# Cross network on one core: a two-engine eviction, a load on another ring, a bias from a table, and other transfer sizes

## The chip, the cores and the metric

One core of a Trainium2 chip runs the whole kernel. The metric is device time in microseconds (us) from launch to end, lower is better. A profiled execution also has a span: from the first to the last instruction on the core.

The engines are TensorE (PE in the profile; its weight loads are PEld), VectorE (DVE), ScalarE (ACT), GpSimd (POOL) and SyncE (SP). SP computes nothing here; its queue issues transfers. ScalarE's queue can issue transfers too, on a ring of its own, in order with ScalarE's computing instructions. Each engine works its instructions off in program order, and waits where an operand isn't ready.

## The reference

Six layers of a cross network over 4096 rows of 416 values, all in bf16:

```python
B, F, D, L = 4096, 26, 16, 6
Din = min(F * D, 1024)          # 416
x0: (B, Din)   ws: (L, Din, Din)   bs: (L, Din)

def reference(x0, ws, bs):
    x = x0
    for l in range(ws.shape[0]):
        x = x0 * (x @ ws[l] + bs[l]) + x
    return x
```

In the first layer x is x0, so the kernel computes x0 * (x0 @ w + (b + 1)) there and saves the addition.

## The kernel before, in words

**Layout.** In layers 0 to 4 x lies transposed: features on the 128 partitions, rows of the batch along the free dimension. The 416 features are three full blocks of 128 (the tiles XM, index m or k) and a remainder of 32 (XR). The 4096 rows are two half-batches s of 2048, each four groups g of 512 columns (CW). Since the remainder has 32 features only, its four groups of one half-batch lie under each other on the 128 partitions: XR[32g:32g+32, 512s:512s+512]. XRx is the same for one half-batch with its upper and lower halves exchanged. WM holds the weights of the full blocks, WR the 32 remainder rows of the weights four times under each other, WD the weights from remainder to remainder as a block diagonal.

**How x0 comes in.** Eight transposed loads on SP's queue (load_x0t, L78) fill XM[0], one for each 512 rows: (s, g) = (0,0), (0,1), ... (1,3). The remainder can't come that way. load_xrem (L83) loads it in three parts, in rows of 64 bytes, into xrem: rows 0 to 1023 on SP (64 KB), rows 1024 to 2047 on ScalarE's ring (64 KB, L275), and the third part, the whole second half-batch, on SP between the sixth and the seventh transposed load (128 KB, L116). x0_rem (L157 to L160) then transposes a part on VectorE in squares of 32 (xrem to xrt), copies it into XR in the right order, and copies XR's halves into XRx.

**First layer** (first_layer, L226 to L272). For each half-batch the columns are handled in two halves h, of two groups each. A block m of a half takes two of the eight PSUM banks (two_banks hands them out in the order of first_order). full (L232) runs three matmuls for each group, row (L239) adds the remainder's part from XR or XRx. Then the banks are emptied. split_first does it with both engines: ScalarE reads the first bank with the bias added (L178), VectorE reads the second with bias and multiplication in one instruction (L179), then multiplies ScalarE's half with x0 (L181). ew_main does it in one piece: ScalarE reads both banks (L166), VectorE multiplies (L169). Block 0 goes through split_first, blocks 2 and 1 through ew_main. The bank pair of block 0 and that of block 2 of the first half are the ones that blocks 1 and 2 of the second half take next. After the second half of the first half-batch, x0_rem(1, 0, 128) stands on VectorE ahead of the evictions of blocks 1 and 2.

**Layers 1 to 4.** Tiles (s, m), each four banks, with matmuls 32 columns wide in four column groups of TensorE (mm_full, L197), the remainder's rows (mm_row, L203) and the remainder's own output (mm_rem, L209 and L214). ScalarE empties two banks at a time with the bias (L166), VectorE multiplies with x0 (L171) and adds x (L172). In layer 4 each finished block is transposed back to rows by a transfer on SP (xl_dmat, L221) into XLrows.

**Last layer.** Here x is the stationary operand, so that rows come out on the partitions. Eight quads q of 4 x 128 rows: full matmuls (mm_q_full, L342), remainder rows (L351) and the bias (L356), which is a matmul with one row: ones times bLr, the last layer's biases, which a small load puts on partitions 0, 32, 64 and 96 (L125). ew_pair empties two groups at a time (L366), multiplies with X0rows (L367), adds XLrows (L368) and stores 208 KB on SP (L369). X0rows is x0 by rows, loaded in one transfer of 3328 KB at the end of SP's loads (L124). The last two quads go through ew_single, a group at a time (L376, L377, L380, L381).

**Small preparations.** bsb holds the six bias rows; VectorE transposes them (L101) and GpSimd spreads them into bM and bR (L103 to L107), then fills WD (L129). Filler matmuls (L146) run on TensorE until the first operands are there.

The order of all instructions is written out by hand; the framework only adds the waits that the operands need.

Of the kernel before, what the change touches and what calls it, by code (L numbers as in the profile page):

```python
# [10 lines left out]
ALU = mybir.AluOpType  # L11
BF16 = mybir.dt.bfloat16
# [4 lines left out]
def kernel(  # L17
# [7 lines left out]
    nc = tc.nc  # L25
    B, D = x0.shape
    L = ws.shape[0]
    P = 128
    NK = 3
    R = D - NK * P  # L30
    assert R == 32 and B == 4096 and D == 416 and L >= 2
    NS = 2
    NG = 4
    CW = 512
    SW = NG * CW
    NBT = B // P
    LL = L - 1
# [11 lines left out]

    dz = const.tile([P, 2], FP32)  # L50
    warm = const.tile([P, CW], BF16)
    ones = const.tile([P, P], BF16)
    WM = const.tile([P, L, NK, D], BF16)
    WR = const.tile([P, L, D], BF16)
    WD = const.tile([P, L, NG, R], BF16)
    bsb = const.tile([R, D], BF16)
    bT = const.tile([R, D // R, R], BF16)
    bLr = const.tile([P, D], BF16)
    bM = const.tile([P, NK, L], FP32)
    bR = const.tile([P, L], FP32)  # L60
    X0rows = big.tile([P, NBT, D], BF16)
    XLrows = big.tile([P, NBT, D], BF16)
    scrR = [big.tile([P, 4, P], BF16, name=f"scrR{s}") for s in range(NS)]
    xrt = [big.tile([P, 16, R], BF16, name=f"xrt{s}") for s in range(NS)]
    xrem = [big.tile([P, 16, R], BF16, name=f"xrem{s}") for s in range(NS)]
    XRx = [big.tile([P, CW], BF16, name=f"XRx{s}") for s in range(NS)]
    XM = [big.tile([P, NK, B], BF16, name=f"XM{i}") for i in range(3)]
    XR = [big.tile([P, NS * CW], BF16, name=f"XR{i}") for i in range(3)]
# [12 lines left out]
    def load_xrem(eng, s, p0, p1):  # L81
        with nc.allow_non_contiguous_dma(reason="64B row segments"):
            eng.dma_start(xrem[s][p0:p1], x0[SW * s + 16 * p0:SW * s + 16 * p1, NK * P:D].rearrange("(p t) r -> p t r", t=16))  # L83
# [4 lines left out]
    nc.vector.memset(warm[:, 0:P], 0.5)  # L88
    nc.vector.memset(warm[:, P:CW], 0.5)
    nc.vector.memset(dz[:], 0.0)  # L90
    nc.gpsimd.memset(bsb[:], 0.0)
    nc.gpsimd.memset(ones[:], 1.0)
    nc.gpsimd.memset(WD[:], 0.0)

    load_x0t(0, 0)
# [2 lines left out]
    load_wr(nc.scalar, 0, 0, 1)  # L98
    nc.scalar.activation(dz[:, 1:2], dz[:, 0:1], ACT.Identity, bias=dz[:, 0:1], scale=1.0)

    nc.vector.transpose(out=bT[:], in_=bsb.rearrange("p (c r) -> p c r", r=R))  # L101
    for q in range(4):
        nc.gpsimd.tensor_copy(bM[32 * q:32 * q + 32, :, :], bT[:, q:4 * NK:4, 0:L])  # L103
    nc.gpsimd.tensor_scalar(out=bM[:, :, 0:1], in0=bM[:, :, 0:1], scalar1=1.0, scalar2=None, op0=ALU.add)
    for g in range(NG):
        nc.gpsimd.tensor_copy(bR[32 * g:32 * g + 32, :], bT[:, 4 * NK, 0:L])
    nc.gpsimd.tensor_scalar(out=bR[:, 0:1], in0=bR[:, 0:1], scalar1=1.0, scalar2=None, op0=ALU.add)  # L107
    for g in range(1, NG):
        nc.vector.tensor_copy(WR[32 * g:32 * g + 32, 0, :], WR[0:32, 0, :])
    load_x0t(0, 1)  # L110
# [2 lines left out]
    load_x0t(0, 3)  # L113
    load_x0t(1, 0)
    load_x0t(1, 1)
    load_xrem(nc.sync, 1, 0, 128)  # L116
    load_x0t(1, 2)
    load_x0t(1, 3)
    load_wm(nc.sync, 1)
# [1 line left out]
        load_wr(nc.sync, g, 1, L)  # L121
    for l in range(2, L):
        load_wm(nc.sync, l)
    nc.sync.dma_start(X0rows[:], x0_v)  # L124
    nc.sync.dma_start(bLr[0:P:32, :], bs[LL:LL + 1, :].broadcast_to([NG, D]))  # L125

    def fill_wd(l0, l1):
        for g in range(NG):
# [24 lines left out]
    def x0_rem(s, p0, p1, parts):  # L153
        XRv = XR[0][p0:p1, CW * s:CW * s + CW].rearrange("p (j t) -> p j t", t=16)
        n = 16 // len(parts)
        for a, copy in enumerate(parts):
            nc.vector.transpose(out=xrt[s][p0:p1, n * a:n * a + n, :], in_=xrem[s][p0:p1, n * a:n * a + n, :])  # L157
            copy(XRv[:, :, n * a:n * a + n], xrt[s][p0:p1, n * a:n * a + n, :].rearrange("p t j -> p j t"))
        for a in range(p0, p1, 64):
            nc.vector.tensor_copy(XRx[s][64 - a:128 - a, :], XR[0][a:a + 64, CW * s:CW * s + CW])  # L160


    def ew_main(l, s, m, h, pt, cur, nxt):
        c0 = col0(s, 2 * h)
        t = tpool.tile([P, 2 * CW], BF16, name="t")
        nc.scalar.activation(t[:], pt.rearrange("p a b -> p (a b)"), ACT.Identity, bias=bM[:, m, l:l + 1], scale=1.0)  # L166
        x0c = XM[0][:, m, c0:c0 + 2 * CW]
        if l == 0:
            nc.vector.tensor_tensor(out=nxt[:, m, c0:c0 + 2 * CW], in0=t[:], in1=x0c, op=ALU.mult)  # L169
            return  # L170
        nc.vector.tensor_tensor(out=t[:], in0=t[:], in1=x0c, op=ALU.mult)  # L171
        nc.vector.tensor_tensor(out=nxt[:, m, c0:c0 + 2 * CW], in0=t[:], in1=cur[:, m, c0:c0 + 2 * CW], op=ALU.add)  # L172


    def split_first(s, m, h, pt, nxt):
        c0 = col0(s, 2 * h)
        t = tpool.tile([P, 2 * CW], BF16, name="t")
        nc.scalar.activation(t[:, 0:CW], pt[:, 0, :], ACT.Identity, bias=bM[:, m, 0:1], scale=1.0)  # L178
        nc.vector.scalar_tensor_tensor(out=nxt[:, m, c0 + CW:c0 + 2 * CW], in0=pt[:, 1, :], scalar=bM[:, m, 0:1],  # L179
                                       in1=XM[0][:, m, c0 + CW:c0 + 2 * CW], op0=ALU.add, op1=ALU.mult)  # L180
        nc.vector.tensor_tensor(out=nxt[:, m, c0:c0 + CW], in0=t[:, 0:CW], in1=XM[0][:, m, c0:c0 + CW], op=ALU.mult)  # L181

    def ew_rem(l, s, pr, curR, nxtR):
        tr = tpool.tile([P, 2 * CW], BF16, name="t")
# [41 lines left out]
    def first_layer(s):  # L226
        cur, nxt = XM[0], XM[1]

        def full(pt, m, h, gl, first, last):
            c0 = col0(s, 2 * h + gl)  # L230
            for k in range(NK):
                nc.tensor.matmul(pt[:, gl, :], lhsT=WM[:, 0, k, 128 * m:128 * m + 128], rhs=cur[:, k, c0:c0 + CW],  # L232
                                 start=(first and k == 0), stop=(last and k == NK - 1), skip_group_check=True)

        def row(pt, m, h, swapped, first):
            for gl in range(2):
                r0 = 32 * ((2 * h + gl + 2 * swapped) % 4)
                src = XRx[s][r0:r0 + 32, :] if swapped else XR[0][r0:r0 + 32, CW * s:CW * s + CW]
                nc.tensor.matmul(pt[:, gl, :], lhsT=WR[r0:r0 + 32, 0, 128 * m:128 * m + 128], rhs=src,  # L239
                                 start=first, stop=(not first), tile_position=(r0, 0), skip_group_check=True)  # L240

        pa = [two_banks() for m in range(NK)]
        for m, gl in ((0, 0), (1, 0), (2, 0), (0, 1), (1, 1), (2, 1)) if s == 0 else ((0, 0), (1, 0), (0, 1), (1, 1), (2, 0), (2, 1)):
            full(pa[m], m, 0, gl, True, False)
        pb = [two_banks()]
        row(pa[0], 0, 0, 0, False)
        if s == 1:
            row(pb[0], 0, 1, 0, True)
        row(pa[2], 2, 0, 0, False)
        row(pa[1], 1, 0, 1, False)  # L250
        split_first(s, 0, 0, pa[0], nxt)
        if s == 0:
            x0_rem(0, 64, 128, (nc.vector.tensor_copy,))
        for m in (2, 1):
            ew_main(0, s, m, 0, pa[m], cur, nxt)
        pb += [two_banks() for m in range(1, NK)]
        for m, gl in ((0, 0), (1, 0), (2, 0), (0, 1), (1, 1), (2, 1)) if s == 0 else ((0, 0), (1, 0), (0, 1), (1, 1), (2, 0), (2, 1)):
            full(pb[m], m, 1, gl, s == 0 or m > 0, s == 1 and m == 0)
            if s == 1 and (m, gl) == (0, 1):
                ew_main(0, s, 0, 1, pb[0], cur, nxt)  # L260
        if s == 0:
            row(pb[0], 0, 1, 0, False)
            row(pb[1], 1, 1, 0, False)
            row(pb[2], 2, 1, 1, False)
            split_first(s, 0, 1, pb[0], nxt)
            x0_rem(1, 0, 128, (nc.vector.tensor_copy,))
            for m in range(1, NK):
                ew_main(0, s, m, 1, pb[m], cur, nxt)
        else:
            row(pb[1], 1, 1, 0, False)  # L270
            row(pb[2], 2, 1, 1, False)
            rem_first(pb)  # L272
# [74 lines left out]
    def mm_q_rows(qs, pys, begun):  # L347
        for q, py in zip(qs, pys):
            s, i = quads[q]
            for g in range(NG):  # L350
                nc.tensor.matmul(py[g // 2][:, g % 2, 0:D], lhsT=curR[32 * g:32 * g + 32, CW * s + 128 * i:CW * s + 128 * i + 128],  # L351
                                 rhs=WR[32 * g:32 * g + 32, l, :], start=not (q == begun and g < 2), stop=False,
                                 tile_position=(32 * g, 0), skip_group_check=True)
        for q, py in zip(qs, pys):
            for g in range(NG):
                nc.tensor.matmul(py[g // 2][:, g % 2, 0:D], lhsT=ones[32 * g:32 * g + 1, :],  # L356
                                 rhs=bLr[32 * g:32 * g + 1, :], start=False, stop=(q == begun and g < 2), tile_position=(32 * g, 0),
                                 skip_group_check=True)

    def ew_pair(q, h, py):  # L360
        s, i = quads[q]
        b0 = 16 * s + 8 * h + i
        t = tpool.tile([P, 2 * CW], BF16, name="t")
        tv = t[:, 0:2 * D].rearrange("p (a d) -> p a d", a=2)
        o = opool.tile([P, 2, D], BF16, name="o")
        nc.scalar.copy(tv, py[h][:, :, 0:D])  # L366
        nc.vector.tensor_tensor(out=tv, in0=tv, in1=X0rows[:, b0:b0 + 5:4, :], op=ALU.mult)  # L367
        nc.vector.tensor_tensor(out=o[:], in0=tv, in1=XLrows[:, b0:b0 + 5:4, :], op=ALU.add)  # L368
        nc.sync.dma_start(out_v[:, b0:b0 + 5:4, :], o[:])  # L369

    def ew_single(q, g, py):
        s, i = quads[q]
# [64 lines left out]
```

## Time and profile before

| | |
|---|---|
| three runs | 130.89, 131.26, 131.39 us; median 131.26 |
| the profiled execution | 130.53 us |
| its span, first to last instruction | 128.7 us |
| granted TensorE clock | 1.0 |
| TensorE busy | 122.9 us, 95% of the span |
| VectorE busy | 104.2 us, 81% |
| ScalarE busy | 83.3 us, 65% |
| GpSimd busy | 7.0 us, 5% |
| largest groups | L197 on TensorE 65.2 us; L166 on ScalarE 59.1 us; L171 and L172 on VectorE 33.3 and 33.5 us |

The busy shares of TensorE, VectorE, ScalarE and the transfers, in 40 slices of 3.2 us each (a digit is tenths, 9 is 90% or more):

```profile
PE   6999999999999999999999999999999999999950
...
DVE  1344969457979898989898989898989999999990
ACT  2117358399757759766749666849666877567760
...
DMA  3989989999991000000000000000398899995663
```

The transfer engines are full from 3 to 38 us, while x0, the weights and X0rows come in, and busy again from 90 us on, with the transposes back and the stores. A group's line names its source line, engine and operation, what it writes from what it reads, how many there are, busy time in us and the mean of one in ns. In the timeline the first two columns are the start and the length in us; instructions of one kind that follow each other are merged into one line (x2 and so on). "Issued" is the moment an engine's queue starts a transfer, "landed" the moment at which whoever waits for it may go on.

### The profile page before, as it was taken

Reading aid. Unit: us, or ns where it says so; the run is one execution under the profiler, and the core shown is the slowest. Engines: PE = TensorE matmul, PEld = TensorE weight load, DVE = VectorE, ACT = ScalarE, POOL = GpSimd, SP = SyncE. Lnnn points to the kernel's source line nnn. Section 1 sums busy time; section 2 is a strip of 40 time slices with the busy share of each in tenths; the row PEclk is TensorE's granted clock in tenths of the full one; section 3 lists DMA queues with packets and bytes.
Section 4 is the critical chain, followed back from the end, with each engine's and each line's share of the span. In section 5 each row is a group of like instructions: output and inputs, shape, how many; then the busy total and the mean of one; then the engine's idle time right before and its main releaser. Section 6 shows DMA issues by size and latency. Waiting matters only on the chain.

```text
span 128.7 us, 3923 instructions
## 1 busy us (share of the span) xinstructions
PE 122.9 (95%) x1677; PEld 54.5 (42%) x1677; DVE 104.2 (81%) x187; ACT 83.3 (65%) x93; POOL 7.0 (5%) x27
## 2 busy tenths in 40 slices
PE   6999999999999999999999999999999999999950
PEld 3343334444434444544444444434444445544420
DVE  1344969457979898989898989898989999999990
ACT  2117358399757759766749666849666877567760
POOL 4250000030000000000000000000000300000000
PEclk9999999999999999999999999999999999999999
DMA  3989989999991000000000000000398899995663
GB/s 94 261 155 222 179 153 277 225 326 333 335 316 30 5 0 8 0 0 5 0 5 0 5 0 5 0 0 5 73 135 185 163 150 234 235 293 176 198 192 103
DMA packets 41973, 16.37 MB, mean 127 GB/s; under 512 B 30778, under 2 KB 41956, under 8 KB 41956
## 3 DMA queue, kind: packets, MB, share of 16 engines
q1 hardware_dynamic: 40456, 15.70, 54.8%
q10 hardware_dynamic: 1500, 0.42, 1.6%
q8 instruction: 13, 0.21, 0.7%
q14 instruction: 4, 0.03, 0.1%
HBM read 6.15 MB, written 3.41 MB: 74 GB/s over the span
## 4 chain that ended last, share of the span: by engine, by line
PE 93%; ACT 2%; DVE 2%; issue 1%; DVEq 0%; ACTq 0%
PE PS L197 49%; PE PS L342 12%; PE PS L232 12%; PE PS L203 5%; PE PS L214 5%; PE PS L146 4%; PE PS L209 2%; PE PS L351 2%; PE PS L239 1%; PE PS L356 1%; DVE t L377 1%; ACT t L166 1%; DVE o L380 1%; ACT t L178 1%; ACT t L376 0%
## 5 line engine op out<-in xcount | busy, mean ns | idle before, releaser
L166 ACT ACTIVATE t<-PS,bM 128x1024 bf16<-128x1024 f32 x57 | 59.1, 1115 | 21.2 <-PE PS L203 21.2
L197 PE MATMUL PS<-XM,WM 128*32 128x512 bf16 x1152 | 65.2, 379 | 0.0
L197 PEld LDWEIGHTS <-WM 128*32 128x32 bf16 x1152 | 29.8, 97 | 33.7 <-issue 5.1
L171 DVE TENSOR_TENSOR t<-t,XM 128x1024 bf16<-128x1024 bf16 x48 | 33.3, 694 | 4.2 <-ACT t L166 4.2
L172 DVE TENSOR_TENSOR XM<-t,XM 128x1024 bf16<-128x1024 bf16 x48 | 33.5, 698 | 3.1
L342 PE MATMUL PS<-WM,XM 128*128 128x416 bf16 x96 | 17.9, 340 | 0.0
L232 PE MATMUL PS<-XM,WM 128*128 128x512 bf16 x72 | 16.9, 385 | 0.2 <-ACT t L166 0.2
L366 ACT CAST t<-PS 128x832 bf16<-128x832 f32 x12 | 10.2, 852 | 5.0 <-PE PS L342 2.3
L342 PEld LDWEIGHTS <-XM 128*128 128x128 bf16 x96 | 8.9, 98 | 8.7 <-issue 2.2
L232 PEld LDWEIGHTS <-WM 128*128 128x128 bf16 x72 | 6.9, 99 | 10.1 <-issue 2.8
L214 PE MATMUL PS<-XM,WM 128*32 128x512 bf16 x120 | 8.2, 379 | 0.0
L185 ACT ACTIVATE t<-PS,bR 128x512 bf16<-128x512 f32 x10 | 6.8, 694 | 2.0 <-POOL WD L129 2.0
L368 DVE TENSOR_TENSOR o<-t,XLrows 128x832 bf16<-128x832 bf16 x12 | 7.1, 592 | 0.5
L203 PE MATMUL PS<-XR,WR 32*128 32x512 bf16 x96 | 7.3, 379 | 0.0
L169 DVE TENSOR_TENSOR XM<-t,XM 128x1024 bf16<-128x1024 bf16 x9 | 5.9, 688 | 1.5 <-ACT t L166 1.5
L367 DVE TENSOR_TENSOR t<-t,X0rows 128x832 bf16<-128x832 bf16 x12 | 7.0, 584 | 0.0
L146 PE MATMUL PS<-warm 128*128 128x512 bf16 (+2 forms) x13 | 4.6, 535 | 1.0 <-DVE warm L88 1.0
L178 ACT ACTIVATE t<-PS,bM 128x512 bf16<-128x512 f32 x3 | 2.1, 687 | 5.3 <-PE PS L239 5.3
L285 POOL COPY XLrows<-scrR 128x512 bf16<-128x512 bf16 x2 | 1.3, 666 | 72.7 <-DMA scrR<-XR 72.7
L157 DVE STREAM_TRANSPOSE xrt<-xrem 64x256 bf16<-64x256 bf16 (+2 forms) x4 | 2.2, 562 | 3.5 <-DMA xrem<-in_x_dram 3.5
L376 ACT CAST t<-PS 128x416 bf16<-128x416 f32 x8 | 4.0, 506 | 1.0 <-PE PS L342 0.8
L214 PEld LDWEIGHTS <-WM 128*32 128x32 bf16 x120 | 3.2, 97 | 3.2
(40 smaller groups left out, 48.1 us busy)
## 6 DMA issues: line engine op xcount, KB each, us to landing
X0rows<-in_x_dram SPq DMA_DIRECT2D x1, 3328.0 KB, 15.3
out_dram<-o SPq DMA_DIRECT2D x12, 208.0 KB, 2.6
WM<-in_ws_dram SPq DMA_DIRECT2D x5, 312.0 KB, 6.5
out_dram<-o SPq DMA_DIRECT2D x8, 104.0 KB, 1.7
WR<-in_ws_dram SPq DMA_DIRECT2D x4, 130.0 KB, 6.0
WM<-in_ws_dram ACTq DMA_DIRECT2D x1, 312.0 KB
XM<-in_x_dram SPq DMA_TRANSPOSE x8, 4.8
xrem<-in_x_dram SPq DMA_DIRECT2D x1, 128.0 KB, 4.4
```

The source lines that it names most:

```text
L146: nc.tensor.matmul(PS[:, 0, 0:cols], lhsT=warm[:, 0:P], rhs=warm[:, 0:cols], start=True, stop=True, skip_group_check=True)
L166: nc.scalar.activation(t[:], pt.rearrange("p a b -> p (a b)"), ACT.Identity, bias=bM[:, m, l:l + 1], scale=1.0)
L171: nc.vector.tensor_tensor(out=t[:], in0=t[:], in1=x0c, op=ALU.mult)
L172: nc.vector.tensor_tensor(out=nxt[:, m, c0:c0 + 2 * CW], in0=t[:], in1=cur[:, m, c0:c0 + 2 * CW], op=ALU.add)
L197: nc.tensor.matmul(pts[g // 2][32 * q:32 * q + 32, g % 2, :], lhsT=WM[:, l, k, 128 * m + 32 * q:128 * m + 32 * q + 32], rhs=cur[:, k, c0:c ...
L203: nc.tensor.matmul(pts[g // 2][:, g % 2, :], lhsT=WR[32 * g:32 * g + 32, l, 128 * m:128 * m + 128], rhs=curR[32 * g:32 * g + 32, CW * s:CW ...
L214: nc.tensor.matmul(pr[32 * g:32 * g + 32, :], lhsT=WM[:, l, k, NK * P:D], rhs=cur[:, k, c0:c0 + CW], start=False, stop=(k == NK - 1), tile ...
L232: nc.tensor.matmul(pt[:, gl, :], lhsT=WM[:, 0, k, 128 * m:128 * m + 128], rhs=cur[:, k, c0:c0 + CW], start=(first and k == 0), stop=(last ...
L342: nc.tensor.matmul(py[g // 2][:, g % 2, 0:D], lhsT=cur[:, k, q_cols(q, g)], rhs=WM[:, l, k, :], start=(first and k == 0), stop=((not first ...
L366: nc.scalar.copy(tv, py[h][:, :, 0:D])
L367: nc.vector.tensor_tensor(out=tv, in0=tv, in1=X0rows[:, b0:b0 + 5:4, :], op=ALU.mult)
L368: nc.vector.tensor_tensor(out=o[:], in0=tv, in1=XLrows[:, b0:b0 + 5:4, :], op=ALU.add)
```

## The change

It has five parts.

- In the first layer's first half of the first half-batch, blocks 0 and 2 both go through split_first, and block 1 through ew_main behind them (before: block 0 split, blocks 2 and 1 in one piece). split_first now returns its last multiplication, so that VectorE reads both banks out of PSUM before it multiplies ScalarE's halves.
- The remainder's third part is issued by ScalarE, behind its eviction of block 1, and no longer by SP between the transposed loads. The two xrem tiles become one.
- The last layer's bias comes from bsb: GpSimd copies its 32 rows to all four groups of 32 partitions, and a table pick[1], in which row 5 of each group of 32 is ones and all others zeros, picks the last layer's row in a matmul of 32 rows. ones, bLr and its load go. VectorE makes pick with two memsets and a transpose.
- X0rows is loaded in eight transfers of 416 KB.
- Quads 0 to 2 are stored in one transfer of 416 KB each.

```diff
-    ones = const.tile([P, P], BF16)
+    pick = [const.tile([P, P], BF16, name=f"pick{i}") for i in range(2)]
...
-    bsb = const.tile([R, D], BF16)
+    bsb = const.tile([P, D], BF16)
...
-    bLr = const.tile([P, D], BF16)
...
-    xrem = [big.tile([P, 16, R], BF16, name=f"xrem{s}") for s in range(NS)]
+    xrem_tile = big.tile([P, 16, R], BF16)
+    xrem = [xrem_tile] * NS
...
-    nc.gpsimd.memset(bsb[:], 0.0)
-    nc.gpsimd.memset(ones[:], 1.0)
+    nc.gpsimd.memset(bsb[0:R, :], 0.0)
+
+    nc.vector.memset(pick[0][:], 0.0)
+    nc.vector.memset(pick[0][:, LL:P:R], 1.0)
+    nc.vector.transpose(out=pick[1][:], in_=pick[0][:])
...
+    for g in range(1, NG):
+        nc.gpsimd.tensor_copy(bsb[32 * g:32 * g + 32, :], bsb[0:R, :])
     for g in range(1, NG):
         nc.vector.tensor_copy(WR[32 * g:32 * g + 32, 0, :], WR[0:32, 0, :])
...
     load_x0t(1, 1)
-    load_xrem(nc.sync, 1, 0, 128)
     load_x0t(1, 2)
...
-    nc.sync.dma_start(X0rows[:], x0_v)
-    nc.sync.dma_start(bLr[0:P:32, :], bs[LL:LL + 1, :].broadcast_to([NG, D]))
+    for q in range(8):
+        nc.sync.dma_start(X0rows[:, 4 * q:4 * q + 4, :], x0_v[:, 4 * q:4 * q + 4, :])
...
-        nc.vector.tensor_tensor(out=nxt[:, m, c0:c0 + CW], in0=t[:, 0:CW], in1=XM[0][:, m, c0:c0 + CW], op=ALU.mult)
+        return lambda: nc.vector.tensor_tensor(out=nxt[:, m, c0:c0 + CW], in0=t[:, 0:CW], in1=XM[0][:, m, c0:c0 + CW], op=ALU.mult)
...
-        split_first(s, 0, 0, pa[0], nxt)
         if s == 0:
+            closing = [split_first(s, m, 0, pa[m], nxt) for m in (0, 2)]
+            for close in closing:
+                close()
             x0_rem(0, 64, 128, (nc.vector.tensor_copy,))
-        for m in (2, 1):
-            ew_main(0, s, m, 0, pa[m], cur, nxt)
+            ew_main(0, s, 1, 0, pa[1], cur, nxt)
+            load_xrem(nc.scalar, 1, 0, 128)
+        else:
+            split_first(s, 0, 0, pa[0], nxt)()
+            for m in (2, 1):
+                ew_main(0, s, m, 0, pa[m], cur, nxt)
...
-                nc.tensor.matmul(py[g // 2][:, g % 2, 0:D], lhsT=ones[32 * g:32 * g + 1, :],
-                                 rhs=bLr[32 * g:32 * g + 1, :], start=False, stop=(q == begun and g < 2), tile_position=(32 * g, 0),
+                nc.tensor.matmul(py[g // 2][:, g % 2, 0:D], lhsT=pick[1][32 * g:32 * g + 32, :],
+                                 rhs=bsb[32 * g:32 * g + 32, :], start=False, stop=(q == begun and g < 2), tile_position=(32 * g, 0),
                                  skip_group_check=True)
+
+    o4 = [big.tile([P, NG, D], BF16, name=f"o4_{q}") for q in range(3)]
...
-        o = opool.tile([P, 2, D], BF16, name="o")
+        o = o4[q][:, 2 * h:2 * h + 2, :] if q < 3 else opool.tile([P, 2, D], BF16, name="o")[:]
...
-        nc.sync.dma_start(out_v[:, b0:b0 + 5:4, :], o[:])
+        if q >= 3:
+            nc.sync.dma_start(out_v[:, b0:b0 + 5:4, :], o)
+        elif h == 1:
+            nc.sync.dma_start(out_v[:, b0 - 8:b0 + 5:4, :], o4[q][:])
```

More of the change, by code (lines that the diff above doesn't have):

```diff
@@ L99 @@
     nc.scalar.activation(dz[:, 1:2], dz[:, 0:1], ACT.Identity, bias=dz[:, 0:1], scale=1.0)
-    nc.vector.transpose(out=bT[:], in_=bsb.rearrange("p (c r) -> p c r", r=R))
+    nc.vector.transpose(out=bT[:], in_=bsb[0:R, :].rearrange("p (c r) -> p c r", r=R))
     for q in range(4):
@@ L264, in first_layer @@
             row(pb[2], 2, 1, 1, False)
-            split_first(s, 0, 1, pb[0], nxt)
+            split_first(s, 0, 1, pb[0], nxt)()
             x0_rem(1, 0, 128, (nc.vector.tensor_copy,))
@@ L364, in ew_pair @@
         tv = t[:, 0:2 * D].rearrange("p (a d) -> p a d", a=2)
-        o = opool.tile([P, 2, D], BF16, name="o")
+        o = o4[q][:, 2 * h:2 * h + 2, :] if q < 3 else opool.tile([P, 2, D], BF16, name="o")[:]
         nc.scalar.copy(tv, py[h][:, :, 0:D])
         nc.vector.tensor_tensor(out=tv, in0=tv, in1=X0rows[:, b0:b0 + 5:4, :], op=ALU.mult)
-        nc.vector.tensor_tensor(out=o[:], in0=tv, in1=XLrows[:, b0:b0 + 5:4, :], op=ALU.add)
-        nc.sync.dma_start(out_v[:, b0:b0 + 5:4, :], o[:])
+        nc.vector.tensor_tensor(out=o, in0=tv, in1=XLrows[:, b0:b0 + 5:4, :], op=ALU.add)
+        if q >= 3:
+            nc.sync.dma_start(out_v[:, b0:b0 + 5:4, :], o)
+        elif h == 1:
+            nc.sync.dma_start(out_v[:, b0 - 8:b0 + 5:4, :], o4[q][:])
     def ew_single(q, g, py):
```

## The prediction

> **What bounds the kernel now.** I read first the page's line of busy times, then the chain of waits in order of time, then the stretch in which that chain leaves TensorE.
>
> ```profile
> PE 122.9 (95%) x1677; PEld 54.5 (42%) x1677; DVE 104.2 (81%) x187; ACT 83.3 (65%) x93; POOL 7.0 (5%) x27
> ```
>
> TensorE is busy for 95% of the span of 128.7 us, at a granted clock of 1.0 throughout. An edit counts only if it changes when TensorE may go on. The chain shows where it may not:
>
> ```profile
> 10.36 0.69 ACT t L178
> 11.05 1.01 ACT t L166
> 12.06 0.04 issue
> 12.11 2.75 PE PS L232 x12
> 14.86 0.54 PE PS L239 x6
> 15.39 3.99 PE PS L232 x18
> 19.38 0.54 PE PS L239 x8
> 19.93 4.14 PE PS L232 x18
> ```
>
> (Columns: start, length, what.) Two losses are in it. First, at 12.11 TensorE has waited for ScalarE to empty the third block's banks (the ACTIVATE of L166 from 11.05). The matmuls of L232 follow each other every 0.216 us and the last before the wait began at about 11.52, so the next was due at 11.74: 0.37 us lost. Second, 18 matmuls of L232 take 3.99 us from 15.39 but 4.14 us from 19.93. The issue of the eighth transposed load of x0 begins at 17.0 and it lands 4.3 us later, at 21.3, where the second half's columns are due at 21.16: 0.15 us lost. After 26 us the chain stays on TensorE to 122.55; then ScalarE and VectorE finish the last single blocks. VectorE has no wait longer than 0.1 us between 95.6 and 123.0, but its last wait before that is for ScalarE, which follows TensorE. So what is won or lost before 26 us moves the rest along and arrives at the end.
>
> Third, I looked at who is nearly late, in the timeline of 8 to 21 us:
>
> ```profile
> 8.40 0.62 ACTq L83 DMA_DIRECT2D xrem<-in_x_dram  x1
> 12.67 0.71 DVE L157 STREAM_TRANSPOSE xrt<-xrem 64x512 bf16<-64x512 bf16 x1 [1.16 <-DMA xrem<-in_x_dram]
> 13.22 0.59 SPq L83 DMA_DIRECT2D xrem<-in_x_dram  x1
> 13.85 4.58 SPq L78 DMA_TRANSPOSE XM<-in_x_dram  x2
> 17.66 0.71 DVE L157 STREAM_TRANSPOSE xrt<-xrem 128x512 bf16<-128x512 bf16 x1 [1.01 <-DMA xrem<-in_x_dram]
> 18.40 0.59 DVE L158 COPY XR<-xrt 128x512 bf16<-128x512 bf16 x1
> 19.03 0.61 DVE L160 COPY XRx<-XR 64x512 bf16<-64x512 bf16 x2
> 19.32 0.60 PE L239 MATMUL PS<-XR,WR 32*128 32x512 bf16 x6
> 19.55 0.38 PE L239 MATMUL PS<-XRx,WR 32*128 32x512 bf16 x2
> ```
>
> This is the pivot. The remainder's third part (the second half-batch's) is issued on SP at 13.22, lands at 17.66, and VectorE turns it into XR (done 18.99) and into the first half of XRx (19.32, half of the 0.61). TensorE uses XR at 19.32 and XRx at 19.55. The load has 0.2 to 0.3 us to spare, no more.
>
> **The change, part by part.**
>
> *Third block evicted by two engines.* ScalarE now takes 512 columns of block 0 and 512 of block 2 (0.69 us each, starts 0.59 apart: 10.36 and 10.95, done 11.64) before block 1. TensorE next needs only the first bank of block 2, so it could go on at 11.74: 0.37 us won. But three matmuls later, at 12.39, it needs the columns of the fourth transposed load. That one is issued at 7.5 and takes 5.1 us to land: 12.6. Before, the use came at 12.76, just behind it. So the wait moves, and 0.12 us is won (bounds: 0 to 0.37, if the load comes sooner). VectorE pays one more SCALAR_TENSOR_TENSOR (0.75) and two half TENSOR_TENSORs (0.43 each) in place of a whole one later (0.69). From 10.39 this ends at about 12.6, as the next part of the remainder lands (12.67), so the transpose behind it is not delayed.
>
> *The remainder's third part on ScalarE's ring.* All parts now share one buffer, so this load must wait for the last reader of the previous one: the VectorE transpose that starts at 12.67 and lasts 0.71. It issues at about 13.43, 0.21 us later than on SP. On ScalarE the waiting issue stands behind block 1's ACTIVATE (done about 12.7) and holds ScalarE to 13.43 and 0.62 more for the issue, to 14.05. Its next work, L178, starts at 15.21 now and at 15.1 then: over 1 us of cover; without that the 0.7 + 0.62 would delay an eviction directly. On SP the two last transposed loads and the weights of layer 1 go 0.63 us sooner, which ends the 0.15 us loss at 21.16.
>
> When does it land? The trace has no 128 KB of 64 B rows on this ring. The nearest row is the second part: the same ring, the same rows, transposed loads in flight on SP, 64 KB: issued 8.40, landed 12.67, 4.27 us. For the other 64 KB, the low bound is the time that its packets took: in the trace's packet records its 1024 packets lie between 10.89 and 11.63, 0.74 us. The high bound is what doubling cost on SP: 3.1 us to landing for 64 KB, 4.4 for 128 KB, 1.3 more. So 5.0 to 5.6 us; I take 5.3, as neither is nearer. Landing: 13.43 + 5.3 = 18.7 (18.4 to 19.0), against 17.66. VectorE is idle by then and needs the same 1.66 us to the first half of XRx, and TensorE starts 0.04 later: 20.40 instead of 19.55, **0.85 us late**. The rows of XR wait too (18.7 + 1.33), so the 0.12 us above is swallowed by this wait. Behind it, VectorE's two TENSOR_TENSORs (1.29) and the SCALAR_TENSOR_TENSOR that frees a bank move by the same amount and stay as far ahead of TensorE as now.
>
> The Trainium skill speaks against the move as such: "DMA: Bandwidth & Descriptors", section "Issuing engines are not separate DMA queues", says that transfers from all issuers share the 16 DMA engines and that another issuer saves only its own issuing time. By it the sum would be that of the second rival below. The 4.27 us for half the size is what speaks against taking the ring as neutral.
>
> *Last biases from a table.* VectorE builds pick: a 128x128 memset (0.17 by L88), a small one (0.06 by L90) and a 128x128 transpose (under the 0.60 of L101's 32x416 one), done by about 2.3; it is idle from 1.39 to 4.64, so nothing, and it would need over 2.4 us more to matter. GpSimd gets three 32x416 copies. By L129 (204 ns for 32 columns, 357 for 160, so 1.2 ns a column) one is 0.66 us: 2.0 in all, from 7.8 to 9.8. The fill of WD behind them ends near 10.7 instead of 8.7; TensorE reads it at 24.3. Their side effect is on VectorE, which makes XR and XRx at 8.72 to 9.49 for a use at 9.88. At 99.66 a VectorE TENSOR_TENSOR of 0.69 took 1.10 under a GpSimd copy; at 5.73 the copies of L109, 260 ns each, ran under GpSimd casts no slower than L160's 288 ns without. At the first ratio 0.66 us of copies become 1.06, and XRx is there at 9.89: nothing to 0.05 lost; I take 0. In the last layer 32 matmuls read 32 rows instead of one. L351 does that in 341 ns, L356 needs 335 for one row; four stand side by side. A run of eight is 0.46 for L351 against 0.35, but L351's is the first after full-height matmuls. Zero, with 0.5 us as the far end over all runs, and VectorE's backlog covers part.
>
> The Trainium skill, "SBUF — State Buffer", section "Who interferes with whom", has it that of a VectorE and a GpSimd instruction that need the shared ports, the later one is blocked for the other's whole length. The 1.10 at 99.66 agrees with a wait of some length, not with a whole one; by the rule the sum would be that of the last rival.
>
> *Sizes.* X0rows in eight loads: eight issues of 0.49 on SP instead of one, and the bias load's issue of 8.32 goes; SP's next work is at 90.95 and X0rows, there by about 41, is first read at 107.22. Three stores of 416 KB for six of 208: three issues of 0.37 less on SP, at 109 to 114, while the end waits for single stores from 121.90 on. Both 0; if the larger stores stood in the way of later ones, 7 us remain to clear them.
>
> *Sum:* 0.85 late at XRx, less 0.15 at 21.16: +0.70 us. The profiled execution took 130.53 (span 128.7 and 1.8 around it), 0.7 under the median of the runs; the difference goes on the median: 131.26 + 0.70 = **132.0 us** (131.7 to 132.3 from the bounds of the landing).
>
> **The rivals.**
>
> *The load stands behind the transposed load issued just before it.* The seventh now begins at 13.22 and ScalarE's load 0.21 us later. For it: the packets of the 64 KB on this ring came out (10.89 to 11.63) just as those of the fourth transposed load ended and before the fifth's began. Against it: the bias rows, issued at 1.20 on this ring, came out at 3.8, in the middle of the first's. Transposed loads land 2.0 apart, so the seventh at 18.4, and 1.2 later the remainder (as 17.66 follows the sixth's 16.4): 19.6, so 1.75 late, less 0.15: +1.6, 132.9 us.
>
> *The ring is neutral, and it isn't slower.* The load takes the 4.43 us it took on SP: landing at 17.86, XRx used at 19.56 as before, and the 0.15 us at 21.16 is won: 131.1 us. For it: on SP it stood behind the sixth transposed load, on ScalarE's ring nothing is ahead. Against it: 4.27 us for half of it there. It decides when the load takes less than 4.6 us; under 4.2 the 0.12 us shows too, and with an earlier fourth load all 0.37: 130.7. By "Queues, rings and completion order" on the same page of the skill the engines take turns between rings packet by packet, which also leaves the load free of the seventh; no run here shows how many packets a turn has.
>
> *GpSimd's copies hold VectorE up at 8.7 to 9.5.* If one of its copies there stands still for a whole GpSimd copy (0.66 by L129), XRx is ready at 9.49 + 0.66 = 10.15 for a use at 9.88: 0.3 us on top of the forecast, 132.3 us. The row at 99.66 speaks for a hold, L109's at 5.73 against it.
>
> **How the numbers follow.** Forecast 0.48, behind the seventh load 0.20, neutral ring 0.24, GpSimd 0.08. A measurement of this kernel tells about 0.5% (0.66 us) from no change; the three runs spread over 0.5 us. Slower by more (over 131.92): 0.29 of the forecast, all of the first rival, 0.06 of the last: 0.55. Faster by more needs the neutral ring with all 0.37 and the runs' spread: 0.11. Within: 0.34. The range holds the far ends of the rivals, 130.9 to 132.9.
>
> **What would show it.** Right: VectorE waits for the load until 18.4 to 19.0; the rows of L239 begin near 20.0 and those of XRx near 20.4; the 18 matmuls after them take 4.0; at 12.1 the wait of TensorE for ScalarE is gone and a short one for a transposed load follows. Wrong: a landing by 17.9, rows at 19.2 to 19.4, or a new gap of TensorE outside 9 to 24 us.

## The result, and the profile after

| kernel | median of 12 runs | lowest to highest | profiled execution, span |
|---|---|---|---|
| before | 130.99 us | 130.65 to 132.12 | 130.53, 128.7 |
| changed | 132.30 us | 131.70 to 134.06 | 132.96, 131.2 |

The changed kernel is slower: the ratio is 1.0092, with a 95% interval of 1.0066 to 1.0119. That is 1.2 us, where 0.7 was forecast and 132.0 us for the whole. Three executions, of the changed kernel (134.06 us), of e3 below (444.0) and of e5 (214.4), ran slower than the rest of their kernel and count in no ratio. The two profiled executions lie 2.4 us apart, because the one of the kernel before is under its median (by 0.5) and that of the changed one over it (by 0.7). So the traces show about twice the loss that the ratio gives, and how the load lands in an execution at the median is not known.

The page's line of busy times of the changed kernel:

```profile
PE 122.7 (94%) x1677; PEld 54.7 (42%) x1677; DVE 105.6 (81%) x191; ACT 82.8 (63%) x93; POOL 9.5 (7%) x29
```

TensorE does the same work (122.7 us against 122.9) in a longer span: the loss is waiting. Who waited for whom, for TensorE alone (columns: total us, times, longest us), first one line of before, then the changed kernel:

```profile
PE PS L232 <- ACT t L166: 0.2, 1, 0.2
```

```profile
PE PS L243 <- DVE XR L162: 1.8, 1, 1.8
PE PS L150 <- DVE warm L88: 1.0, 1, 1.0
PE PS L236 <- DMA XM<-in_x_dram: 1.0, 3, 0.5
```

Before, the list held the 1.0 us at the start and these 0.2 us for ScalarE (L166). That second entry is gone; in its place stand three short waits for transposed loads and one of 1.8 us for XR. The chain of waits in the stretch of 4 to 30 us leads from XR to its cause (columns: start, length, what):

```profile
8.80 4.30 DMA xrem_tile<-in_x_dram
13.10 0.02 issue
13.13 0.72 DVE xrt L161
13.85 0.02 issue
13.87 6.71 DMA xrem_tile<-in_x_dram
20.57 0.02 issue
20.60 0.72 DVE xrt L161
21.32 0.02 issue
21.34 0.60 DVE XR L162
21.95 0.04 issue
21.99 0.71 PE PS L243 x8
22.70 4.02 PE PS L236 x18
```

In the kernel before, this stretch of the chain was TensorE throughout. Now the remainder's third part is on it for 6.71 us, and ahead of that, linked by the shared buffer, the second part and its transpose. The timeline of the changed kernel, with the same instructions as shown of before:

```profile
8.80 0.63 ACTq L83 DMA_DIRECT2D xrem_tile<-in_x_dram  x1
13.12 2.10 PE L236 MATMUL PS<-XM,WM 128*128 128x512 bf16 x9 [0.50 <-DMA XM<-in_x_dram]
13.13 0.71 DVE L161 STREAM_TRANSPOSE xrt<-xrem_tile 64x512 bf16<-64x512 bf16 x1 [0.66 <-DMA xrem_tile<-in_x_dram]
13.87 0.58 ACTq L83 DMA_DIRECT2D xrem_tile<-in_x_dram  x1
20.60 0.71 DVE L161 STREAM_TRANSPOSE xrt<-xrem_tile 128x512 bf16<-128x512 bf16 x1 [3.87 <-DMA xrem_tile<-in_x_dram]
21.34 0.59 DVE L162 COPY XR<-xrt 128x512 bf16<-128x512 bf16 x1
21.97 0.61 DVE L164 COPY XRx<-XR 64x512 bf16<-64x512 bf16 x2
21.99 0.61 PE L243 MATMUL PS<-XR,WR 32*128 32x512 bf16 x6 [1.83 <-DVE XR L162]
22.31 0.39 PE L243 MATMUL PS<-XRx,WR 32*128 32x512 bf16 x2
```

XRx is used at 22.31 instead of 19.55. TensorE ends 2.65 us later (126.74 against 124.09), so nothing of it is made up behind 26 us. The program's close, from VectorE's last instruction to the end of the span, is 0.2 us shorter.

The seventh transposed load was issued on SP 0.23 us ahead of the third part (13.64). It was slower too: from issue to landing before, and in the changed kernel:

```profile
DMA to landing us min/median/max: 5.8/5.8/5.8
DMA to landing us min/median/max: 7.0/7.0/7.0
```

So in the changed kernel the two loads landed together, at 20.6 us.

### The profile page after: what moved, and what is told of

Its sections match the earlier page's. It is cut to its first block, busy times and chain, and to the rows that moved or that the text cites. A ratio compares the mean times of both kernels' runs of the same rounds, so it can differ in the third digit from the quotient of the medians.

```text
span 131.2 us, 3928 instructions
## 1 busy us (share of the span) xinstructions
PE 122.7 (94%) x1677; PEld 54.7 (42%) x1677; DVE 105.6 (81%) x191; ACT 82.8 (63%) x93; POOL 9.5 (7%) x29
## 3 DMA queue, kind: packets, MB, share of 16 engines
HBM read 6.15 MB, written 3.41 MB: 73 GB/s over the span
## 4 chain that ended last, share of the span: by engine, by line
PE 79%; DMA 11%; DVE 4%; SPq 3%; issue 0%; ACT 0%; DVEq 0%
PE PS L201 48%; PE PS L352 12%; DMA xrem_tile<-in_x_dram 11%; PE PS L207 5%; PE PS L218 5%; SPq L78 3%; PE PS L236 3%; PE PS L213 2%; PE PS L361 2%; DVE xrt L161 1%; DVE t L392 1%; PE PS L366 1%; PE PS L243 1%; DVE o L395 1%; DVE XR L162 0%
## 5 line engine op out<-in xcount | busy, mean ns | idle before, releaser
L170 ACT ACTIVATE t<-PS,bM 128x1024 bf16<-128x1024 f32 x56 | 58.1, 1114 | 21.3 <-PE PS L207 21.3
L182 ACT ACTIVATE t<-PS,bM 128x512 bf16<-128x512 f32 x4 | 2.6, 685 | 8.1 <-PE PS L243 8.1
L161 DVE STREAM_TRANSPOSE xrt<-xrem_tile 64x256 bf16<-64x256 bf16 (+2 forms) x4 | 2.2, 562 | 6.1 <-DMA xrem_tile<-in_x_dram 6.1
```

## The experiments

Each ratio is to the kernel before, run on the same chip, with its 95% interval. There were 12 executions of each, but 6 of e2, e6, e7 and e11 and 4 of e5.

| kernel | median, us | ratio (interval) |
|---|---|---|
| e1 changed, third part back on SP | 130.56 | 0.9979 (0.9965 to 0.9994) |
| e2 before, ring alone | 132.19 | 1.0125 (1.0086 to 1.0165) |
| e3 changed, a buffer of its own | 131.32 | 1.0026 (1.0006 to 1.0046) |
| e4 before, eviction alone | 130.72 | 0.9990 (0.9976 to 1.0003) |
| e5 changed, SP silent behind the load | 136.59 | 1.0449 (1.0417 to 1.0481) |
| e6 before, table alone | 131.23 | 1.0046 (1.0028 to 1.0065) |
| e7 before, sizes alone | 131.35 | 1.0053 (1.0036 to 1.0070) |
| e8 e1, GpSimd's copies later | 130.51 | 0.9981 (0.9966 to 0.9997) |
| e9 before, table and sizes | 130.55 | 0.9987 (0.9973 to 1.0001) |
| e10 before, eight loads alone | 130.81 | 1.0010 (0.9998 to 1.0021) |
| e11 before, larger stores alone | 131.18 | 1.0036 (1.0022 to 1.0050) |

### Is it the ring? Taken out of the changed kernel (e1), and put alone into the one before (e2)

e1, against the changed kernel:

```diff
-    xrem_tile = big.tile([P, 16, R], BF16)
-    xrem = [xrem_tile] * NS
+    xrem = [big.tile([P, 16, R], BF16, name=f"xrem{s}") for s in range(NS)]
...
     load_x0t(1, 1)
+    load_xrem(nc.sync, 1, 0, 128)
...
             ew_main(0, s, 1, 0, pa[1], cur, nxt)
-            load_xrem(nc.scalar, 1, 0, 128)
```

> The changed kernel with the remainder's third part back on SP between the sixth and the seventh transposed load, with its own buffer; all else as changed. Theory (the late landing of this load is the whole loss): VectorE waits for it until 17.7 to 18.2 as in the kernel before, TensorE's rows of the second half-batch begin at 19.3 to 19.6, and the time is 130.6 to 131.2 us, a ratio of 0.997 to 1.002. Rival (GpSimd's copies beside VectorE, or another of the parts, cost a good part of it): 131.5 us or more, ratio above 1.004.

e2, against the kernel before:

```diff
-    xrem = [big.tile([P, 16, R], BF16, name=f"xrem{s}") for s in range(NS)]
+    xrem_tile = big.tile([P, 16, R], BF16)
+    xrem = [xrem_tile] * NS
...
-    load_xrem(nc.sync, 1, 0, 128)
...
             ew_main(0, s, m, 0, pa[m], cur, nxt)
+        if s == 0:
+            load_xrem(nc.scalar, 1, 0, 128)
```

> The kernel before with one part alone: the remainder's third part in the shared buffer, issued by ScalarE behind the evictions of blocks 2 and 1. Theory: it lands 6 to 7 us after its issue, TensorE loses 1 to 2 us ahead of the rows of the second half-batch, and the time is 132.0 to 132.8 us, ratio 1.008 to 1.014. Rival (the ring is neutral and the loss lies in the other parts): landing 4.5 to 5 us after issue, ratio 0.999 to 1.003.

e1 is 0.2% faster than the kernel before and e2 1.25% slower; both ratios lie where the theory had them. The whole loss of the changed kernel goes with this one part, the ring and the shared buffer together; the rival for e1 falls. The timeline of e2:

```profile
14.32 0.57 ACTq L84 DMA_DIRECT2D xrem_tile<-in_x_dram  x1
19.61 0.71 DVE L157 STREAM_TRANSPOSE xrt<-xrem_tile 128x512 bf16<-128x512 bf16 x1 [2.05 <-DMA xrem_tile<-in_x_dram]
21.00 0.61 PE L239 MATMUL PS<-XR,WR 32*128 32x512 bf16 x6 [1.33 <-DVE XR L158]
```

The load lands 5.3 us after its issue, sooner than the 6 to 7 that the theory had, but the issue is late, since the second part's transpose, for which it waits, began at 13.58 in this execution. In e1's timeline, with the load on SP, it lands 4.55 us after its issue at 13.64, and TensorE's wait is nearly gone:

```profile
18.22 0.71 DVE L161 STREAM_TRANSPOSE xrt<-xrem 128x512 bf16<-128x512 bf16 x1 [1.51 <-DMA xrem<-in_x_dram]
19.61 0.61 PE L243 MATMUL PS<-XR,WR 32*128 32x512 bf16 x6 [0.18 <-DVE XR L162]
```

### Why does it land late? Issued earlier (e3), and with SP silent (e5)

e3 gives the third part a buffer of its own and leaves it on ScalarE's ring; the diff is the first three lines of e1's.

> The changed kernel with a buffer of its own for the third part, still on ScalarE's ring at the same place: the load no longer waits for VectorE's transpose and issues at about 12.7, ahead of the seventh transposed load (13.2 to 13.6) and no longer behind it. Theory of order (a load on ScalarE's ring comes out behind the transposed load whose issue began last): its packets follow the sixth transposed load's and it lands at 17.0 to 18.2; TensorE waits under 0.4 us; 130.7 to 131.4 us, ratio 0.998 to 1.004. Rival (on this ring the load takes 6 to 7 us wherever it starts): landing at 19.0 to 19.6, ratio 1.004 to 1.008. Rival two (the shared buffer's wait on ScalarE costs, not the landing): TensorE waits for ScalarE's evictions in the changed kernel and not here.

e3's timeline:

```profile
11.67 0.57 ACTq L82 DMA_DIRECT2D xrem<-in_x_dram  x1
17.32 0.71 DVE L160 STREAM_TRANSPOSE xrt<-xrem 128x512 bf16<-128x512 bf16 x1 [0.35 <-DMA xrem<-in_x_dram]
17.60 2.75 PE L235 MATMUL PS<-XM,WM 128*128 128x512 bf16 x12 [0.50 <-DMA XM<-in_x_dram]
```

The load was issued at 11.67, a microsecond sooner than expected, since ScalarE issues it while its last eviction still runs. It lands at 17.3, in time, and the loss shrinks to 0.26%; TensorE waits 0.50 us at 17.60 for the sixth transposed load (0.25 in the changed kernel), into whose transfer the remainder's packets now fall, which is more than the theory allowed. The buffer alone is the difference between this kernel and the changed one: of the 1.13% between the changed kernel and e1, about 0.66 go with sharing it, and 0.47 are left for the ring. The landing lies in the range of the theory of order, the rival's 19.0 to 19.6 is missed. But 5.6 us from issue to landing is long, and the first packet came at 14.61, when 60% of the sixth transposed load's packets (13.69 to 15.52) had gone, and not behind them, so this run does not settle the order. Rival two falls: neither here nor in the changed kernel does TensorE wait for ScalarE.

e5, against the changed kernel, takes SP's loads away:

```diff
-    load_x0t(1, 2)
-    load_x0t(1, 3)
-    load_wm(nc.sync, 1)
...
+    def late_loads():
+        load_xrem(nc.sync, 0, 0, 8)
+        load_x0t(1, 2)
+        load_x0t(1, 3)
+        load_wm(nc.sync, 1)
...
             x0_rem(1, 0, 128, (nc.vector.tensor_copy,))
+            late_loads()
```

> The changed kernel, but SP issues nothing between the sixth transposed load and VectorE's transpose of the third part: the transposed loads 7 and 8 and all later loads stand behind a small reload of 8 partitions of the shared remainder buffer (its values are read by nobody), which waits for that transpose. The load on ScalarE's ring is issued as before, at 13.4 to 14.3, with no transposed load begun ahead of it that is not nearly done. Theory of order (on ScalarE's ring it came out behind the seventh transposed load): now its packets begin within 2.2 us of its issue, right behind the sixth's (15.1 to 15.5), and it lands 3.5 to 4.6 us after issue. Rival (the ring needs about 3 us to the first packet and 5.3 to 6.7 to landing by itself): first packet 2.9 to 3.4 us after issue, landing 5.0 us or more. The time itself gets worse under both, 134 us or more, since loads 7 and 8 come late.

```profile
13.91 0.57 ACTq L83 DMA_DIRECT2D xrem_tile<-in_x_dram  x1
17.92 0.71 DVE L163 STREAM_TRANSPOSE xrt<-xrem_tile 128x512 bf16<-128x512 bf16 x1 [1.18 <-DMA xrem_tile<-in_x_dram]
18.66 0.82 SPq L83 DMA_DIRECT2D xrem_tile<-in_x_dram  x1
```

This timeline of e5 is to be held against that of the changed kernel: the issue is at the same time (13.91 against 13.87), but the load lands after 4.0 us and not after 6.71. In the trace's packet records its first packet comes 1.65 us after the issue, as the sixth transposed load's last ones go (15.82); in the changed kernel it comes after 3.41 us, at 17.28. So the rival falls: by itself the ring doesn't need that long. What was taken away are the seventh transposed load, issued at 13.64, 0.23 us ahead, and the eighth, issued at 15.68, also before that first packet. With them on SP the load on ScalarE's ring came out late.

Whether it stood behind the seventh is not shown. In e2 the packets fit that (issued 14.32, packets from 17.30, the seventh's last at 17.56), and so do those of the second part in the kernel before (10.89, the fourth's last at 11.16). But in the changed kernel, as in e3, the first packet came in the middle: at 17.28, 690 of the seventh's 1536 packets (15.48 to 18.85) had gone, and until 18.5 both loads' packets came out side by side. The records don't say which of the 16 transfer engines took a packet, so each engine may have kept the order, or have taken turns. What the runs do show is the size: beside SP's transposed loads this load took 5.3, 5.6 and 6.7 us on ScalarE's ring (e2, e3, changed kernel), 4.4 and 4.55 in its place on SP (before, e1), and 4.0 on ScalarE's ring with SP silent.

### The other parts alone (e4, e6, e7, e9, e10, e11), and one of them moved (e8)

e4 is the kernel before with the eviction's part of the change; its diff is the lines of split_first and first_layer shown of the change, without the load.

> The kernel before with the two-engine eviction of block 2 alone. Theory: the wait of TensorE for ScalarE at 12.1 goes, three matmuls later TensorE waits for the fourth transposed load, 0.1 us is won: 130.8 to 131.1 us, ratio 0.998 to 1.001. Rival (the transposed load is there in time): the whole 0.37 us, ratio 0.996 to 0.998, with no wait for a transposed load near 12.4.

```profile
PE PS L232 <- DMA XM<-in_x_dram: 0.5, 1, 0.5
```

In e4 this line takes the place of TensorE's wait for ScalarE: the wait moves to the fourth transposed load, as forecast. The ratio of 0.9990 leaves 0.1 us, or nothing; in the traces the matmuls that need this load begin at 12.84 in e4 and at 12.76 before, so there nothing is won.

e6 is the kernel before with the lines of pick, bsb, ones and bLr.

> The kernel before with the bias table alone. Theory: GpSimd's copies of bsb stretch VectorE's copy into XR from 0.37 to 0.6 or more, the rows of the first half begin up to 0.3 us later, and as nothing else hides it there the kernel loses 0.1 to 0.3 us: ratio 1.0005 to 1.0025. Rival (as the prediction took it, nothing): 0.999 to 1.0005.

e7 is the kernel before with the lines of X0rows and of the stores; e10 has the first alone, e11 the second alone.

> The kernel before with the eight loads of X0rows and the three larger stores alone. Theory: nothing, ratio 0.9985 to 1.0015, TensorE's chain as before from 26 us on. Rival (the larger stores delay the later ones, or the eight loads delay weights): 1.002 or more.

Both lost about 0.5%, more than either theory allowed. e7's ratio is in its rival's range. In e6 the copy was stretched as expected. Its timeline:

```profile
9.08 0.62 DVE L161 COPY XR<-xrt 64x256 bf16<-64x256 bf16 x1
9.81 0.29 DVE L163 COPY XRx<-XR 64x512 bf16<-64x512 bf16 x1
```

VectorE's copy into XR takes 0.62 instead of 0.37. But by their traces both kernels end TensorE's work 0.2 to 0.3 us later than the kernel before and lose 0.44 to 0.5 more behind VectorE's last instruction: 3.44 us to the end of the span in e6, 3.5 in e7, 3.00 before. The first of these need not come from the edits: e11 below, which leaves everything ahead of the stores as it was, also ends TensorE's work 0.27 us later, with a wait of 0.38 us for a transposed load at 5.68. The changed kernel and e1, e3 and e8 need only 2.74 to 2.80 behind VectorE's last instruction, but e5, which has all five parts too, needs 3.38. So the losses need not add, which e9 to e11 tested:

> The kernel before with the bias table, the eight loads of X0rows and the three larger stores, that is, everything but the eviction and the ring. Alone the table cost 0.46% and the sizes 0.53%, most of it, by their traces, behind VectorE's last instruction (3.4 to 3.5 us to the end of the span against 3.0), while the kernels with all of them end 2.75 to 2.8 us behind it. Theory (the ends do not add: the close of the program costs what the program as a whole makes of it): 2.7 to 3.0 us behind VectorE's last instruction, ratio 0.998 to 1.002. Rival (the parts add, and the eviction paid for them): ratio 1.007 to 1.012.

> The kernel before with X0rows in eight loads alone. Theory: nothing up to VectorE's last instruction beyond 0.3 us of spread in how the loads of x0 land; any loss over that sits behind it. Ratio 0.999 to 1.005. Rival (the eight loads delay weights or XLrows): TensorE or VectorE waits for a DMA after 25 us.

> The kernel before with the three larger stores alone. Theory: nothing, ratio 0.999 to 1.002. Rival (the larger stores are what cost 0.5% with the eight loads): ratio 1.003 to 1.006, with the single stores at the end landing later than 1.7 us after issue.

They don't add: table and sizes together are at 0.9987, with 2.75 us behind VectorE's last instruction. The larger stores alone cost 0.36%, against e11's theory, with 3.46 us there, and the eight loads alone 0.1%, with 3.14 and an interval that holds no change. The single stores of e11 land in 1.7 us as before, so e11's rival, in the way it was put, falls too. What SP waits for at the close, in e11 and in e9:

```profile
SPq L437 <- DMA out_dram<-o: 1.3, 1, 1.3
```

```profile
SPq L441 <- DMA out_dram<-o: 0.7, 2, 0.4
```

The wait for the last stores is 0.6 us shorter in e9. That doesn't order the closes, though: in the kernel before this line has 1.4 us, with 3.00 at the close. In e7 SP also issues the last store 0.6 us after VectorE's end (126.64 against 126.04), and 0.2 before. Why the close is long in one program and short in another stays open.

e8, against e1:

```diff
-    for g in range(1, NG):
-        nc.gpsimd.tensor_copy(bsb[32 * g:32 * g + 32, :], bsb[0:R, :])
...
     fill_wd(1, L)
+    for g in range(1, NG):
+        nc.gpsimd.tensor_copy(bsb[32 * g:32 * g + 32, :], bsb[0:R, :])
```

> The changed kernel with the third part back on SP (own buffer) and GpSimd's three copies of bsb behind its last fill of WD, so that they run at 25 to 30 us and not at 8 to 9.5. Theory: VectorE's copy into XR takes 0.37 again and the rows of the first half begin 0.1 to 0.3 us earlier, but TensorE then waits for the fourth transposed load, so that little shows: 130.4 to 130.7 us, ratio 0.996 to 0.999. Rival (the copies were worth their full stretch): 0.996 or less.

```profile
8.76 0.37 DVE L160 COPY XR<-xrt 64x256 bf16<-64x256 bf16 x1
```

That copy is back at 0.37 in e8's timeline (0.69 in e1), the rows of the first half begin at 9.51 instead of 10.15, and the time is the same within the intervals (0.9981 and 0.9979). What covers the stretch are later waits: in e8 TensorE waits 0.4 us for a transposed load and then, as in e1, for XR from the third part (0.28 at 19.48; 0.18 at 19.61 in e1). e1 and e8 beat both kernels, the one before by 0.2%.

## Why the prediction was right, and where its sizes were off

**Direction and place: right.** The rows of the second half-batch wait for the remainder's third part, which lands late on ScalarE's ring. e1 and e2 show that this part is the whole loss. That the time came within 0.3 us of the forecast is partly luck: of the signs that were named, the landing (20.57, not 18.4 to 19.0), the rows (21.99, not 20.0) and XRx (22.31, not 20.4) all came later in the trace, and the traced loss is 2.4 us.

**The landing: the mechanism of the forecast held, its size was too small.** Issue was put at 13.43 and the load at 5.3 us. In the changed kernel's trace the issue was at 13.87, because the second part landed at 13.10 and not at 12.67 (0.44), and the load took 6.71 (1.41 more). With the 0.85 forecast for XRx this makes 2.70; measured were 2.76. In e2 the issue was 0.89 late and the load took 5.3, the forecast's number; e3's 5.6 is its upper bound. The term that was too small was the landing's upper bound of 5.6, scaled from the 64 KB row. That row's 4.27 us are 2.49 to the first packet, 0.75 for the packets and 1.03 behind them. In the changed kernel the three are 3.41, 2.04 and 1.26: the packets took the 1.3 us more of the upper bound, and the time to the first packet, taken as the same, grew by 0.92.

**The shared buffer: seen, but not its weight.** The forecast had the wait for VectorE's transpose, as 0.21 us against the issue on SP. e3 shows what a buffer of its own allows on the ring: an issue at 11.67 and most of the loss gone.

**The first rival was right in part.** SP's transposed loads do hold the load up; e5 shows it. That it stands behind the whole seventh is not shown: in the trace its packets begin in the middle of the seventh's, and the two land together, where the rival had 1.2 us between them (18.4 and 19.6). The rival's 132.9 us was too much for the median, its landing too early for the trace, and it had been given 0.20. The measured 132.3 lies between the two cases.

**The neutral ring fell.** A ring that only saves issuing time would have left the load at 4.4 us. The Trainium skill's rule ("DMA: Bandwidth & Descriptors", section "Issuing engines are not separate DMA queues") was right that another ring brings no faster transfer, and the trace adds a loss to it. That the rings take turns packet by packet, as the same page of the Trainium skill has it in its section "Queues, rings and completion order", doesn't by itself explain 3.41 us to the first packet against 1.65 with SP silent. Why the first packet comes late stays open.

**The eviction: right in place, its gain not shown.** The wait for ScalarE goes and reappears as one for the fourth transposed load; 0.12 us was forecast, e4 gives 0.1 with zero in its interval. The 0.15 us at the eighth transposed load is won (the 18 matmuls behind the rows take 4.02 us, against 4.14), but not because that load comes sooner: it lands at 21.7, 0.4 later than before, and TensorE comes to it later still.

**The copies on GpSimd: taken at nothing, and nothing in the time, but not for the reason given.** VectorE's copy was stretched in the changed kernel, e1 and e6 (0.62 to 0.69 against 0.37), by under half of the 0.66 that the rival on GpSimd's copies had. What hides it are the later waits, for the fourth transposed load, which the forecast had worked out for the eviction and not used here, and for the third part.

**Sizes and table at the close: missed in kind.** The forecast named no cost or gain behind VectorE's last instruction. Alone these parts cost 0.46% and 0.53%; in the changed kernel the close is 0.2 us shorter than before. What sets its length stays open.

## What to carry to other kernels

Look at what is in flight beside a load, not only at what queue it is issued on: on a ring of its own beside transposed loads it took 5.3 to 6.7 us here, more than the 4.4 to 4.6 in line with them, and a buffer shared to save space can push its issue late. When loads land one behind the other just in time, taking away a wait of the computing engines only uncovers the next load; read the landing times before pricing such an edit. Parts measured alone need not add up, so leave one part out of the whole as well as putting it in alone.

## What the runs showed of the hardware that was not expected

- 128 KB in rows of 64 bytes on ScalarE's ring: 6.71 us from issue to landing with transposed loads issued on SP (one 0.23 us ahead, one 1.8 behind), 4.0 us with SP silent. The packets themselves took 1.7 to 2.0 us. The transposed load issued just ahead took 7.0 us, against 5.8 before.
- A VectorE copy of 64x256 took 0.62 to 0.69 us under GpSimd's copies in the changed kernel, e1 and e6, and 0.37 without them. With the same copies it took 0.41 in e3, and 0.37 in e5 and e9, where the copy behind it (64x512, from XR to XRx) took 0.45 instead of 0.29.
- From VectorE's last instruction to the end of the span it was 2.74 to 3.5 us, with the same last stores, depending on edits far from the end.
